# Where the first tiles of x are transposed: tile 1 moved from a transposing load to TensorE, the first loads spread over two queues, and the transposing loads of tiles 2 and 3 put behind a wait

## The chip, the cores and the metric

The kernel runs on one core of a Trainium2 chip. The metric is the device time of one execution in microseconds (us); lower is better. Before the change the median of three runs is 273.49 us (273.46 to 273.66).

## What is computed

One block of a network over 2048 tokens of width 640: a linear attention with 32 heads of width 20 (A), a gated feed-forward of width 1728 (B), and a gate per token that mixes both. All inputs are bfloat16.

```python
def _A_ref(x, wqkv, wo):
    B, S, D = x.shape                      # 1, 2048, 640
    H = 32; Dh = D // H
    qkv = (x @ wqkv).reshape(B, S, 3, H, Dh).transpose(2, 0, 3, 1, 4)
    q, k, v = qkv[0], qkv[1], qkv[2]
    phi = lambda t: jnp.where(t > 0, t + 1, jnp.exp(t)) + 1e-6
    pq, pk = phi(q), phi(k)
    kv = jnp.einsum("bhsd,bhse->bhde", pk, v)
    z = jnp.einsum("bhsd->bhd", pk)
    num = jnp.einsum("bhqd,bhde->bhqe", pq, kv)
    den = jnp.einsum("bhqd,bhd->bhq", pq, z)[..., None] + 1e-6
    return (num / den).transpose(0, 2, 1, 3).reshape(B, S, D) @ wo

def _B_ref(x, w_gate, w_up, w_down):
    return (_gelu(x @ w_gate) * (x @ w_up)) @ w_down

g = _sigmoid((x * gate_w).sum(-1, keepdims=True))
out = g * _A_ref(x, wqkv, wo) + (1 - g) * _B_ref(x, w_gate, w_up, w_down)
```

## The kernel before

The tokens are cut into 16 tiles of 128 (`i`, 0 to 15), and the width of 640 into 5 chunks of 128 (`k`, 0 to 4). TensorE contracts over the 128 partitions, so it needs x with the width on the partitions: `xT`, a buffer of 5 chunks by 2048 tokens. `x_aug` holds x as it lies in memory, tokens on the partitions; it is read later, by the products that sum over the tokens.

The program is written through a small planner. `P.op(engine, function, reads, writes)` appends an instruction to one engine's list, in the order of the calls, and works out which semaphores it must wait for from the resources that it reads and writes. Each engine runs its list strictly in order, and a DMA is an entry of the list of the engine that issues it: "sp" by default, "act" where it is said. An SP instruction that waits holds every later DMA of SP back. SP's DMAs and ACT's DMAs form two queues (q1 and q10 in the profile).

**The loads, in SP's order (L368 to L400).** `load_x(i)` is a plain load of one tile into `x_aug`, `load_wk(k)` a plain load of one chunk of the key weights (both 160 KB, issued at L343), `load_xT(i)` a transposing load of one tile straight into `xT` (L355), `load_wq(k)` a chunk of the query weights. Before: SP issues x0, wk0, xT1, wk3, wk4, xT2, xT3, the five wq, xT4 to xT15, then the rest of x into `x_aug` in two bulk loads, the feed-forward weights and others. ACT issues a tiny load (L368), wk1, wk2, then runs one Exp (which loads its table) and issues the load of the gate vector. `load_xT` already has a parameter `after`, resources that must be there before it is issued; before, nobody passes it.

**NXN** is the number of tiles that are loaded plainly and transposed by TensorE: tile 0 alone. `T(i, ks, tb)` (L435) transposes chunks `ks` of tile i into PSUM bank `tb` with one matmul each against an identity (L439) and copies them to `xT` on DVE (L443). It is called twice a tile, for chunk 0 and for chunks 1 to 4, so that the product with chunk 0 may start after the first, small copy (`r_xTa`).

**The first stage on TensorE (L510 to L534).** `warm(count, n)` issues matmuls of constants whose result nobody reads (bank 4). `KM(n, ks)` (L451) multiplies chunks `ks` of tile n by the key weights, per chunk one matmul of 512 columns (L459) and one of 128 (L460), into the two PSUM banks of slot n (`SLOTS`: banks 0 and 1, 2 and 3, 4 and 5, 6 and 7). `gate_col()` puts the gate vector beside the query weights (one tiny matmul, L504, and a copy). The order is T(0), then KM of tile 0 for chunks 0 to 2, of tile 1 for chunks 0 to 2, both for chunk 3, the gate, both for chunk 4; then tile 2, tile 3, and `QM`, the query products of tiles 0 to 3. `phi1` (ACT, L484) and `phi2` (DVE, L494 and L498) turn each slot into the features.

**Afterwards** `KQ(i)` (L537) does keys and queries of tiles 4 to 15 (matmuls at L544), `MM` (L594) the sums over tokens (L601 to L617), `G` (L694) the feed-forward with the attention's small products between, and `O_tile` and its relatives (L826 to L886) the output.

Of the kernel before, what the change touches and what calls it, by code (L numbers as in the profile page):

```python
# [16 lines left out]
KC = D // 128  # L17
# [3 lines left out]
EPS = 1e-6  # L21
XW = 656

NXN = 1
NQ = 4


# [135 lines left out]
def bass_gated_mix__linear_attn_block__geglu_ffn__prompt_kernel(  # L163
# [63 lines left out]
    with (  # L227
# [8 lines left out]
        with contextlib.ExitStack() as stack:  # L236
# [12 lines left out]
            def new_dma_key():  # L249
                k = "in%d" % dma_next[0]  # L250
                dma_next[0] += 1
                return k
# [16 lines left out]
            wk = wkq[:, :, 0:640]  # L269
# [38 lines left out]
            r_xT = [P.sb("xT%d" % i, R_XT, R_XT + KC * S) for i in range(NT)]  # L308
            r_xTa = [P.sb("xTa%d" % i, R_XT, R_XT + S) for i in range(NXN)]
            r_wk = [P.sb("wk%d" % k, R_WK + k * WW, R_WK + k * WW + 640) for k in range(KC)]  # L310
# [31 lines left out]
            def dma_in(dst, src, writes, reads=(), eng="sp"):  # L342
                P.op(eng, lambda e, dst=dst, src=src: e.dma_start(dst, src),  # L343
                     reads=reads, writes=writes, dma=new_dma_key())
# [3 lines left out]
            def load_x(i, eng="sp"):  # L348
                dma_in(x_aug[:, i, 0:640], A_x[0, i * 128:(i + 1) * 128, :], [r_xn[i]], eng=eng)

            def load_wk(k, eng="sp", after=()):
                dma_in(wk[:, k, :], A_wqkv[k * 128:(k + 1) * 128, 640:1280], [r_wk[k]], reads=after, eng=eng)

            def load_xT(i, after=()):
                P.op("sp", lambda e: e.dma_start_transpose(xT[:, :, i * 128:(i + 1) * 128],  # L355
                                                           A_x[0, i * 128:(i + 1) * 128, :]),
                     reads=list(after), writes=[r_xT[i]], dma=new_dma_key())

            def load_wq(k, eng="sp"):
# [8 lines left out]
            P.op("act", lambda e: e.dma_start(touch[0:16, 0:4], A_wqkv[0:128:8, 640:644]),  # L368
                 writes=[P.res("touch")], dma=new_dma_key())
            load_x(0)  # L370
            load_wk(0)
            load_xT(1)
            load_wk(3)
            load_wk(4)
            load_wk(1, "act")
            load_wk(2, "act")

            zero = nc.const_aps.tensor(0.0, (128, 1), F32)
            P.op("act", lambda e: e.activation(eg[:, 0:1], zero, ACT.Exp), writes=[r_eg[0]])
            P.op("dve", lambda e: e.memset(gw_sb, 0.0), writes=[r_gw])  # L380
            dma_in(gw_sb[0:5, :], gate_w.rearrange("(k p) -> k p", p=128), [r_gw], eng="act")
            for i in range(2, NQ):
                load_xT(i)
            for k in range(KC):
                load_wq(k)
            for i in range(NQ, NT):
                load_xT(i)
            dma_in(x_aug[:, NXN:8, 0:640],
                   A_x[0, NXN * 128:8 * 128, :].rearrange("(i p) w -> p i w", p=128), r_xn[NXN:8])
            dma_in(x_aug[:, 8:NT, 0:640],  # L390
# [30 lines left out]
            def warm(count, n):  # L421
                def fn(e):
                    last = None
                    for w in range(count):
                        last = e.matmul(ps[:, 4, 0:n], one_l, one_r[:, 0:n], start=True, stop=True)
                    return last
                P.op("pe", fn, writes=[bank[4]])
# [4 lines left out]
            def slot(n):  # L432
                return SLOTS[n % 4]

            def T(i, ks, tb):  # L435
                def fn(e):
                    last = None
                    for n, k in enumerate(ks):
                        last = e.transpose(psb[:, tb, n * 128:(n + 1) * 128],  # L439
                                           x_aug[:, i, k * 128:(k + 1) * 128], ident)  # L440
                    return last
                P.op("pe", fn, reads=[r_xn[i], r_ident], writes=[bank[tb]])
                P.op("dve", lambda e: e.tensor_copy(  # L443
                    xT[:, ks[0]:ks[-1] + 1, i * 128:(i + 1) * 128],
                    psb[:, tb, 0:len(ks) * 128].rearrange("p (k s) -> p k s", k=len(ks))),
                    reads=[bank[tb]], writes=[r_xTa[i] if ks[0] == 0 else r_xT[i]])
# [1 line left out]

            seq = [("k", i) for i in range(NQ)] + [("q", i) for i in range(NQ)]

            def KM(n, ks):  # L451
                i = seq[n][1]
                b0, b1 = slot(n)

                def fn(e):
                    last = None
                    for k in ks:
                        lhs = xT[:, k, i * 128:(i + 1) * 128]
                        e.matmul(ps[:, b0, :], lhs, wk[:, k, 0:512], start=(k == 0), stop=(k == KC - 1))  # L459
                        last = e.matmul(ps[:, b1, 0:128], lhs, wk[:, k, 512:640],  # L460
                                        start=(k == 0), stop=(k == KC - 1))
                    return last
                P.op("pe", fn, reads=[r_xTa[i] if i < NXN and ks == [0] else r_xT[i]] + [r_wk[k] for k in ks],
                     writes=[bank[b0], bank[b1]])

            def QM(n, ks):
                i = seq[n][1]
                b0, b1 = slot(n)

                def fn(e):  # L470
                    last = None
                    for k in ks:
                        lhs = xT[:, k, i * 128:(i + 1) * 128]
                        e.matmul(ps[:, b0, :], lhs, wq[:, k, 0:512], start=(k == 0), stop=(k == KC - 1))  # L474
                        last = e.matmul(ps[:, b1, 0:129], lhs, wq[:, k, 512:641],
                                        start=(k == 0), stop=(k == KC - 1))
                    return last
                P.op("pe", fn, reads=[r_xT[i], r_gcol] + [r_wq[k] for k in ks],
                     writes=[bank[b0], bank[b1]])

            def phi1(n):
                b0, b1 = slot(n)
                m = n % 4
                P.op("act", lambda e: e.activation(e_buf[m], ps_flat[:, b0 * 512:b0 * 512 + 640], ACT.Exp),  # L484
                     reads=[bank[b0], bank[b1]], writes=[r_e[m]])
                kind, i = seq[n]
                if kind == "q":
                    P.op("act", lambda e: e.activation(eg[:, i:i + 1], ps[:, b1, 128:129], ACT.Tanh, scale=0.5),
                         reads=[bank[b1]], writes=[r_eg[i]])

            def phi2(n):
                b0, b1 = slot(n)
                m = n % 4
                P.op("dve", lambda e: e.tensor_scalar(e_buf[m], e_buf[m], 1.0, EPS, ALU.min, ALU.add),  # L494
                     reads=[r_e[m]], writes=[r_e[m]])
                kind, i = seq[n]
                dst, r_dst = (pk[i], r_pk[i]) if kind == "k" else (pq[i], r_pq[i])
                P.op("dve", lambda e: e.scalar_tensor_tensor(  # L498
                    dst, ps_flat[:, b0 * 512:b0 * 512 + 640], 1.0 + EPS, e_buf[m], ALU.add, ALU.max),
                    reads=[bank[b0], bank[b1], r_e[m]], writes=[r_dst])  # L500

            def gate_col():

                P.op("pe", lambda e: e.matmul(ps[:, 7, 0:5], gw_sb, ident[:, 0:5], start=True, stop=True),  # L504
                     reads=[r_gw, r_ident], writes=[bank[7]])
                P.op("dve", lambda e: e.tensor_copy(wq[:, :, 640:641], ps[:, 7, 0:5].unsqueeze(2)),
                     reads=[bank[7]], writes=[r_gcol])
# [3 lines left out]
            T(0, [0], 7)  # L511
            T(0, [1, 2, 3, 4], 6)
            warm(1, 512)
            for k in range(3):
                KM(0, [k])
            for k in range(3):
                KM(1, [k])
            KM(0, [3])
            KM(1, [3])
            gate_col()  # L520
            KM(0, [4])
            KM(1, [4])
            ALLK = list(range(KC))
            for n in range(2 * NQ):
                if n in (2, 3):
                    KM(n, ALLK)
                if n == NQ:
                    for k in ALLK:
                        QM(NQ, [k])
                        QM(NQ + 1, [k])  # L530
                if n > NQ + 1:
                    QM(n, ALLK)
                phi1(n)
                phi2(n)  # L534
# [409 lines left out]
```

## Time and profile before

| | us |
|---|---|
| median of three runs | 273.49 (273.46 to 273.66) |
| the profiled execution | 273.48 |
| its span, first to last instruction | 272.2 |

Busy time of the engines in stretches of the span, from the profiled execution:

| stretch, us | what | TensorE busy | DVE busy | ACT busy | GB/s moved |
|---|---|---|---|---|---|
| 0 to 3 | first loads, warm matmuls | 2.17 | 0.11 | 0.80 | 83 |
| 3 to 4 | T(0) | 1.00 | 0.23 | 0.69 | 323 |
| 4 to 5 | first key chunks | 0.81 | 0.42 | 0.00 | 284 |
| 5 to 7 | key chunks of tiles 0 and 1 | 1.78 | 0.00 | 0.00 | 233 |
| 10.8 to 16.4 | query chunks of tiles 0 to 3 | 5.60 | 4.04 | 2.90 | 147 |
| 16.4 to 48.9 | KQ, tiles 4 to 15 | 32.29 | 28.84 | 17.43 | 283 |
| 48.9 to 272.2 | all the rest | 220.12 | 104.82 | 52.12 | 51 |

The granted TensorE clock is 1.00 in all of them. Busy time is what an engine's instructions cover; matmuls overlap, so a busy TensorE is one that always has a matmul in flight. In the names of the views "PE" is TensorE, "PEld" its weight load, "SPq" and "ACTq" the issue of a DMA on SP and ACT, L343 the line, "pool" the kernel's one SBUF buffer, "ps" PSUM, and in_A_x_dram and in_A_wqkv_dram the inputs x and the attention's weights.

Time from issue to landing of the loads of the first stage (start of the issue on its queue, then the profile's time to landing):

| load | queue | issued | to landing |
|---|---|---|---|
| x0 | SP | 0.79 | 2.2 |
| wk0 | SP | 1.26 | 3.0 |
| tile 1, transposing | SP | 1.71 | 3.8 |
| wk3 | SP | 3.07 | 3.5 |
| wk4 | SP | 3.68 | 3.3 |
| tile 2, transposing | SP | 4.15 | 3.9 |
| tile 3, transposing | SP | about 5.4 | 3.3 |
| wq0 to wq4 | SP | 6.72 to 8.8 | 2.5, 2.8, 2.7, 3.0, 3.4 |
| tile 4, transposing | SP | 9.23 | 3.8 |
| wk1, wk2 | ACT | 1.24 and about 1.7 | 3.2 (median of both) |

### The profile page before, as it was taken

What the parts mean: (1) busy time and instruction counts of PE and PEld (TensorE: products, weight loads), DVE (VectorE), ACT (ScalarE), POOL (GpSimd) and SP (SyncE); (2) the same over time, 40 slices, a digit from 0 to 9 for tenths busy, and PEclk for the clock granted to TensorE, in tenths of its full rate; (3) what the DMA queues carried; (4) which work ended last, traced back from release to release, by engine and by line L of the source; (5) the groups of instructions that cost most, each with busy time, mean ns of one, the idle gap of its engine ahead of it and who ended that gap; (6) DMA issues with size and microseconds to landing.
All of it is one profiled execution on the core that took longest, in us unless ns stands there. A gap on an engine that the chain in (4) does not pass through costs nothing.

```text
span 272.2 us, 3460 instructions
## 1 busy us (share of the span) xinstructions
PE 267.3 (98%) x1365; PEld 127.0 (47%) x1391; DVE 141.0 (52%) x248; ACT 75.9 (28%) x132; POOL 30.6 (11%) x30
## 2 busy tenths in 40 slices
PE   8999999999999999999999999999999999999997
PEld 3555555544445454444444444444444444444444
DVE  1678989997234335999999999634110000000200
ACT  2455555210422453332222232224011122121021
POOL 6000000003240002242332421000000000000000
PEclk9999999999999999999999999999999999999999
DMA  7976999610200011615121221272031110110221
GB/s 189 202 117 126 348 401 381 116 8 19 58 19 2 23 52 48 199 27 48 28 48 30 45 48 25 60 235 92 2 78 40 39 39 19 40 39 19 58 60 39
DMA packets 42680, 23.61 MB, mean 87 GB/s; under 512 B 32167, under 2 KB 41255, under 8 KB 42535
## 3 DMA queue, kind: packets, MB, share of 16 engines
q1 hardware_dynamic: 42333, 23.05, 32.4%
q10 hardware_dynamic: 330, 0.33, 0.4%
q8 instruction: 11, 0.18, 0.3%
q14 instruction: 6, 0.05, 0.1%
HBM read 13.67 MB, written 2.63 MB: 60 GB/s over the span
## 4 chain that ended last, share of the span: by engine, by line
PE 96%; DMA 1%; SPq 1%; issue 1%; DVE 0%
PE ps L705 41%; PE ps L879 23%; PE ps L544 12%; PE ps L601 6%; PE ps L858 4%; PE ps L683 2%; PE ps L474 2%; PE ps L826 2%; PE ps L604 1%; DMA pool<-in_A_x_dram 1%; PE ps L459 1%; PE ps L839 1%; SPq L343 1%; SPq L355 0%; PE ps L754 0%
## 5 line engine op out<-in xcount | busy, mean ns | idle before, releaser
L705 PE MATMUL ps<-pool 128*128 128x512 bf16 x509 | 112.8, 379 | 0.7 <-issue 0.2
L705 PEld LDWEIGHTS ps<-pool 128*128 128x128 bf16 x520 | 50.5, 98 | 60.3
L879 PE MATMUL ps<-pool 128*128 128x512 bf16 (+2 forms) x300 | 62.2, 366 | 0.5 <-issue 0.2
L711 ACT ACTIVATE pool<-ps 128x512 f32<-128x512 f32 x52 | 31.0, 597 | 72.8 <-PE ps L705 70.1
L713 DVE TENSOR_TENSOR pool<-ps,pool 128x512 bf16<-128x512 f32 x52 | 34.7, 689 | 31.1 <-PE ps L705 29.8
L879 PEld LDWEIGHTS ps<-pool 128*128 128x128 bf16 x306 | 29.1, 98 | 33.5 <-issue 0.4
L862 DVE TENSOR_TENSOR pool<-ps,pool 128x512 bf16<-128x512 f32 x4 | 2.8, 692 | 61.5 <-PE ps L858 59.4
L544 PE MATMUL ps<-pool 128*128 128x512 bf16 (+1 forms) x176 | 32.5, 343 | 0.2
L769 POOL TENSOR_TENSOR pool<-pool 128x640 f32<-128x640 bf16 x16 | 22.4, 1404 | 72.6 <-DVE pool L771 65.5
L886 ACT ACTIVATE pool<-ps,pool 128x512 bf16<-128x512 f32 (+1 forms) x16 | 10.9, 680 | 68.6 <-PE ps L879 68.6
L544 PEld LDWEIGHTS ps<-pool 128*128 128x128 bf16 x180 | 17.6, 98 | 15.0
L563 DVE SCALAR_TENSOR_TENSOR pool<-ps,pool 128x128 bf16<-128x128 f32 (+2 forms) x36 | 21.7, 603 | 2.1
L554 ACT ACTIVATE pool<-ps 128x640 bf16<-128x640 f32 x24 | 16.9, 703 | 15.8 <-DVE pool L563 9.4
L601 PE MATMUL ps<-pool 128*128 128x512 bf16 x76 | 19.2, 379 | 0.1
L779 DVE TENSOR_TENSOR pool<-pool 128x640 bf16<-128x640 bf16 x16 | 13.2, 825 | 0.6
L777 DVE TENSOR_SCALAR pool<-pool 128x32 f32<-128x32 f32 x16 | 12.8, 802 | 0.6
L771 DVE TENSOR_REDUCE pool<-pool 128x32 f32<-128x640 f32 x16 | 12.9, 808 | 0.0
L649 DVE TENSOR_TENSOR pool<-pool 128x640 f32<-128x640 f32 x14 | 11.6, 826 | 0.5
L858 PE MATMUL ps<-pool 128*128 128x512 bf16 x51 | 11.4, 379 | 0.0
L651 POOL PARTITION_ALL_REDUCE pool<-pool x1 | 4.0, 3971 | 60.2 <-DVE pool L649 60.2
L601 PEld LDWEIGHTS ps<-pool 128*128 128x128 bf16 x78 | 7.0, 98 | 7.3
L560 DVE TENSOR_SCALAR pool<-pool 128x640 bf16<-128x640 bf16 x24 | 7.9, 327 | 1.7 <-ACT pool L554 0.4
(73 smaller groups left out, 123.6 us busy)
## 6 DMA issues: line engine op xcount, KB each, us to landing
out_dram<-pool SPq DMA_DIRECT2D x19, 128.0 KB, 1.7
pool<-in_B_w_gate_dram SPq DMA_DIRECT2D x1, 2080.0 KB, 14.0
pool<-in_B_w_up_dram SPq DMA_DIRECT2D x1, 2080.0 KB, 18.1
pool<-in_A_wqkv_dram SPq DMA_DIRECT2D x8, 160.0 KB, 3.0
pool<-in_A_x_dram SPq DMA_DIRECT2D x1, 1280.0 KB, 9.1
pool<-in_A_x_dram SPq DMA_DIRECT2D x1, 1120.0 KB, 6.2
pool<-in_B_w_down_dram SPq DMA_DIRECT2D x1, 1120.0 KB, 6.2
pool<-omg_row SPq DMA_DIRECT2D x1, 1024.0 KB, 4.5
```

The costliest lines, as they stand in the source:

```text
L544: last = e.matmul(ps[:, b + p, 0:c1 - c0], xT[:, k, i * 128:(i + 1) * 128], wkq[:, k, c0:c1], start=(k == 0), stop=(k == KC - 1))
L554: P.op("act", lambda e: e.activation(e_buf[m], ps_flat[:, o:o + 640], ACT.Exp), reads=banks, writes=[r_e[m]])
L563: P.op("dve", lambda e, c0=c0, c1=c1: e.scalar_tensor_tensor(dst[:, c0:c1], ps_flat[:, o + c0:o + c1], 1.0 + EPS, e_buf[m][:, c0:c1], ALU. ...
L601: last = e.matmul(ps[:, b, :], pk[i][:, c * 128:(c + 1) * 128], x_aug[:, i, 0:512], start=(i == 0), stop=(i == NT - 1))
L705: last = e.matmul(ps[:, b, :], w[:, k, fc * 128:(fc + 1) * 128], xT[:, k, j * 512:(j + 1) * 512], start=(k == 0), stop=(k == KC - 1))
L711: P.op("act", lambda e: e.activation(ge[n], ps[:, gb, :], ACT.Gelu_apprx_tanh), reads=[bank[gb]], writes=[r_ge[n]])
L713: P.op("dve", lambda e: e.tensor_tensor(hT[fc][:, j * 512:(j + 1) * 512], ps[:, ub, :], ge[n], ALU.mult), reads=[bank[ub], r_ge[n]], write ...
L769: P.op("pool", lambda e: e.tensor_tensor(tmp[n], pq[i], z_b, ALU.mult), reads=[r_pq[i], r_zb], writes=[r_tmp[n]])
L771: P.op("dve", lambda e: e.tensor_reduce(den[n], tmp[n].rearrange("p (h d) -> p h d", h=32), AX.X, ALU.add), reads=[r_tmp[n]], writes=[r_de ...
L779: P.op("dve", lambda e: e.tensor_tensor(pq[i].rearrange("p (h d) -> p h d", h=32), pq[i].rearrange("p (h d) -> p h d", h=32), den[n].unsqu ...
L858: last = e.matmul(ps[:, b, :], wd[:, fc, 512:640], hT[fc][:, j * 512:(j + 1) * 512], start=False, stop=(fc == NFC - 2), skip_group_check=True)
L879: last = e.matmul(ps[:, pb, 0:c1 - c0], lhs, rhs, start=False, stop=(q == len(rows) - 1), skip_group_check=True)
```

## The change

`NXN` becomes 2: tile 1 is loaded plainly into `x_aug`, and TensorE transposes it (two calls of T, banks 5 and 4). Its transposing load goes; the bulk load of `x_aug` starts at tile 2. SP issues x0, wk0, wk2, wk4; ACT issues the tiny load, x1, wk1, wk3. The transposing loads of tiles 2 and 3 now wait for wk0 to have landed before SP issues them; the query chunks and all else on SP come after them as before. On TensorE two short warm matmuls are added, and the chunks of tiles 0 and 1 are taken in the order 0, 2, 1, 4, 3, with T(1) after the first chunk of tile 0; the stop flag of the accumulation goes to the last chunk in the new order, so `KM` has a new parameter.

```diff
--- before.py
+++ after.py
@@ -21,7 +21,7 @@
 EPS = 1e-6
 XW = 656
 
-NXN = 1
+NXN = 2
 NQ = 4
 
 
@@ -368,19 +368,19 @@
             P.op("act", lambda e: e.dma_start(touch[0:16, 0:4], A_wqkv[0:128:8, 640:644]),
                  writes=[P.res("touch")], dma=new_dma_key())
             load_x(0)
+            load_x(1, "act")
             load_wk(0)
-            load_xT(1)
-            load_wk(3)
+            load_wk(1, "act")
+            load_wk(2)
+            load_wk(3, "act")
             load_wk(4)
-            load_wk(1, "act")
-            load_wk(2, "act")
 
             zero = nc.const_aps.tensor(0.0, (128, 1), F32)
             P.op("act", lambda e: e.activation(eg[:, 0:1], zero, ACT.Exp), writes=[r_eg[0]])
             P.op("dve", lambda e: e.memset(gw_sb, 0.0), writes=[r_gw])
             dma_in(gw_sb[0:5, :], gate_w.rearrange("(k p) -> k p", p=128), [r_gw], eng="act")
-            for i in range(2, NQ):
-                load_xT(i)
+            for i in range(NXN, NQ):
+                load_xT(i, [r_wk[0]])
             for k in range(KC):
                 load_wq(k)
             for i in range(NQ, NT):
@@ -448,7 +448,7 @@
 
             seq = [("k", i) for i in range(NQ)] + [("q", i) for i in range(NQ)]
 
-            def KM(n, ks):
+            def KM(n, ks, last_chunk):
                 i = seq[n][1]
                 b0, b1 = slot(n)
 
@@ -456,9 +456,9 @@
                     last = None
                     for k in ks:
                         lhs = xT[:, k, i * 128:(i + 1) * 128]
-                        e.matmul(ps[:, b0, :], lhs, wk[:, k, 0:512], start=(k == 0), stop=(k == KC - 1))
+                        e.matmul(ps[:, b0, :], lhs, wk[:, k, 0:512], start=(k == 0), stop=(last_chunk and k == ks[-1]))
                         last = e.matmul(ps[:, b1, 0:128], lhs, wk[:, k, 512:640],
-                                        start=(k == 0), stop=(k == KC - 1))
+                                        start=(k == 0), stop=(last_chunk and k == ks[-1]))
                     return last
                 P.op("pe", fn, reads=[r_xTa[i] if i < NXN and ks == [0] else r_xT[i]] + [r_wk[k] for k in ks],
                      writes=[bank[b0], bank[b1]])
@@ -511,19 +511,21 @@
             T(0, [0], 7)
             T(0, [1, 2, 3, 4], 6)
             warm(1, 512)
-            for k in range(3):
-                KM(0, [k])
-            for k in range(3):
-                KM(1, [k])
-            KM(0, [3])
-            KM(1, [3])
-            gate_col()
-            KM(0, [4])
-            KM(1, [4])
+            warm(2, 128)
+            KM(0, [0], False)
+            T(1, [0], 5)
+            T(1, [1, 2, 3, 4], 4)
+            KM(0, [2], False)
+            for k in (0, 2, 1, 4, 3):
+                if k in (1, 4, 3):
+                    KM(0, [k], k == 3)
+                KM(1, [k], k == 3)
+                if k == 4:
+                    gate_col()
             ALLK = list(range(KC))
             for n in range(2 * NQ):
                 if n in (2, 3):
-                    KM(n, ALLK)
+                    KM(n, ALLK, True)
                 if n == NQ:
                     for k in ALLK:
                         QM(NQ, [k])
```

## The prediction

> **What bounds the kernel now.** I read the page first, parts 1 and 4: is one engine full, and does the chain that ended last run through it?
>
> ```profile
> PE 267.3 (98%) x1365; PEld 127.0 (47%) x1391; DVE 141.0 (52%) x248; ACT 75.9 (28%) x132; POOL 30.6 (11%) x30
> ...
> PE 96%; DMA 1%; SPq 1%; issue 1%; DVE 0%
> ```
>
> TensorE is busy nearly always and 96% of the chain is its own work. The few per cent that aren't lie at the start, so I read the chain of waits in order of time up to 8.6 us (start, length, what).
>
> ```profile
> 0.79 0.41 SPq L343
> ...
> 1.26 0.41 SPq L343
> ...
> 1.71 1.30 SPq L355
> ...
> 3.07 0.57 SPq L343
> ...
> 3.68 0.43 SPq L343
> ...
> 4.15 3.88 DMA pool<-in_A_x_dram
> ...
> 8.07 0.39 PE ps L459
> ```
>
> The reader is to see that the chain is SP's queue: it issues x0, wk0, the transposing load of tile 1 (1.30 us of issuing against 0.41 for a plain load), wk3 and wk4, and only at 4.15 the transposing load of tile 2. That lands after 3.88 us, and at 8.07 the key product of tile 2 begins. From there TensorE never waits again: the 10 key chunks of tiles 2 and 3 run 8.07 to 10.80, so 0.273 each, and the query chunks follow. So the time changes by as much as the start of tile 2's product moves, unless tile 3 or a query chunk becomes late.
>
> The timeline of TensorE up to there shows its other waits (start, length, instruction, then the idle time of the weight load and its releaser).
>
> ```profile
> 4.34 0.10 PEld L459 LDWEIGHTS ps<-pool 128*128 128x128 bf16 x1 [0.50 <-DVE pool L443]
> ...
> 5.54 0.10 PEld L459 LDWEIGHTS ps<-pool 128*128 128x128 bf16 x1 [0.52 <-DMA pool<-in_A_x_dram]
> ...
> 6.56 0.10 PEld L459 LDWEIGHTS ps<-pool 128*128 128x128 bf16 x1 [0.36 <-DMA pool<-in_A_wqkv_dram]
> ...
> 8.07 0.10 PEld L459 LDWEIGHTS ps<-pool 128*128 128x128 bf16 x1 [0.56 <-DMA pool<-in_A_x_dram]
> ```
>
> The first is put down to the copy of L443, but its two copies began at 3.69 and took 0.23 and 0.43, so the small one was done by 3.92; what came last was wk0, issued at 1.26 and landed 3.0 later, at 4.26. The next is tile 1's transposing load (issued 1.71, 3.8 to land: 5.5), then wk3 (3.07, 3.5: 6.6), then tile 2.
>
> How far could any change of this stage go? From 4.37 on, 20 key chunks at 0.273, five transposes (about 0.45, below) and the gate column (0.03, L504 to the next matmul at 7.12 and 7.15) are 5.94 us: query chunks at 10.31 instead of 10.80. **Without a single wait the gain is 0.5 us**; if the first chunk also started when the small copy ends, 3.92 plus some 0.07, 0.9 us.
>
> **The change part by part.**
>
> *Transposing load of tile 1 taken out.* SP has 1.30 + 0.05 us less to issue, and tile 1 no longer waits until 5.5.
>
> *Plain x1 and the key chunks on two queues.* SP issues x0, wk0, wk2, wk4 at about 0.79, 1.26, 1.71, 2.16; ACT issues x1, wk1, wk3 at about 1.24, 1.69, 2.15, with x1 where wk1 stood. ACT's table load slips from 2.20 to about 2.65 and the gate vector's load with it; ACT then sat idle 3.9 us before its first L484 at 7.62, which hides it. Seven loads of 160 KB (163.8 kB) are 1.15 MB. The windows say 83 GB/s over the first 3.0 us, 0.25 MB; the other 0.90 MB go at 323 GB/s (window 3 to 4, both queues filled) in 2.8 us, last byte at 5.8. Each queue gets half if they share evenly, one load per 1.0 us. With wk0 where it landed before (4.26; its own queue has the same ahead of it) and x1 where wk1 landed (1.24 + 3.2 = 4.44), estimates are wk2 5.25, wk4 6.25, wk1 5.45, wk3 6.45.
>
> *Tile 1 transposed by TensorE (T(1), five transposes), two copies by DVE, two more warm matmuls.* The row of L439 has five in 0.62, before 3.96; one 128-column matmul among the key chunks costs 0.055 at best. So five cost 0.28 to 0.62; I take 0.45, five weight loads of 0.10 less a little, because the load of 0.10 is longer than 0.055 and each transpose has its own. The copies cost 0.23 and 0.43 and start 0.35 after their first transpose (3.34 to 3.69); DVE was idle for 2.93 us before 7.36, so they delay nobody but the chunks of tile 1. The two warm matmuls, about 0.1, lie before wk0 lands.
>
> *New order of the chunks.* KM(0,0) 4.37 to 4.64; T(1) (x1 there at 4.44) to 5.09, small copy done 5.3, large one 5.85; KM(0,2) at 5.28 for wk2, to 5.55; KM(1,0) to 5.82; KM(1,2) after the copy 5.9 to 6.17; then KM(0,1), KM(1,1), KM(0,4), KM(1,4), gate, KM(0,3), KM(1,3): 6 x 0.273 + 0.03 to **7.84**. Each of wk1, wk4, wk3 is there 0.5 to 0.8 before its use. Before, the last of these chunks began at 7.42 and TensorE was free at 7.7; so tile 0 and 1 end about 0.15 later, in the shade of the 8.07. If that shade went, it is 7.84 that would set the start of tile 2.
>
> *The transposing loads of tiles 2 and 3, now behind a wait for wk0.* SP is through with its plain loads at 2.6 and then waits for wk0, to 4.26 + 0.05. Queued behind the wait on SP are both transposing loads, all five query chunks, tiles 4 to 15 and every later load; TensorE waits for the first. So tile 2 is issued at 4.31 against 4.15 before: the 1.5 us saved on SP are all spent waiting. From issue to landing the first three transposing loads took 3.8, 3.9 and 3.3; the first two, like the one to come, had plain chunks ahead of them. In the new order wk4 is some 0.2 us from its end when the descriptors of tile 2 are out (4.31 + 1.30 = 5.6), somewhat less than before, so I take 3.75 with 3.3 and 4.6 (the shortest of the first three, and the longest of all 15) as bounds: landing at **8.06**, bounds 7.6 and 8.9. Tile 3 is issued at 5.65, lands at 8.95 to 9.5 (3.3 to 3.85), and is needed 5 x 0.273 after 8.08, at 9.45. The query chunks are issued 0.16 later each; they landed at 9.2 to 12.1 (6.72 + 2.5 to 8.75 + 3.4) and are used from 10.80 to 12.98, 0.9 or more of slack. Tile 4 (9.23 + 3.8 = 13.0) is used at 16.42.
>
> One row about the price of a transposing load: with the transposing loads of tiles 2 and 3 in the queue the DMA moved less, with plain loads only more.
>
> ```profile
> 7.00:8.00 1.00, 0.85 (x8) 0.33 (x5) 0.18 (x1) 0.38 (x1) 0.00 (x0) 1.00 1.05 160
> 8.00:10.50 2.50, 2.37 (x17) 1.36 (x19) 2.08 (x4) 1.62 (x3) 0.00 (x0) 1.00 0.93 266
> ```
>
> The last numbers are GB/s: 160 and 266. [...]
>
> *The bulk load of x_aug* (1120 KB at 25.5 us) loses one tile; the products that read it begin at 48.9.
>
> Sum: tile 2's product starts at 8.08 instead of 8.07, nothing after it waits: 273.48 of the profiled execution + 0.0 = **273.5 us**. That execution's span is 272.2, 1.3 lie around it, and the median of the runs is 273.49, so no correction.
>
> **The rivals.**
>
> *No wait is left (272.8).* If wk0 lands earlier because no transposing load is being issued in the same microseconds, say at 3.9, SP's wait ends earlier too, tile 2 lands at 3.95 + 3.3 to 3.75, so 7.3 to 7.7, and TensorE's chain decides, itself begun up to 0.4 earlier: 7.4 against 8.07, 272.8. For it: the window of 0 to 3 moved only 83 GB/s, so there is room. Against: wk0 shares the DMA with ACT's first load as before, and x1's landing holds T(1).
>
> *The wait costs more than the load it removes (274.3).* The mechanism is SP held by wk0 with both transposing loads behind it. It decides once tile 2 lands after 8.6, which takes wk0 at 4.8 or a landing time of 4.35. At the longest row, 4.6, tile 2 is there at 8.91, 0.84 late: 274.3; tile 3 at 5.65 + 4.6 = 10.25 would alone cost 0.7. For it: three of the 15 took 4.2 or more by the list of issues, the issue begins later than before by 0.16, and more plain traffic stands on the other queue. Against: those long ones had other transposing loads ahead of them.
>
> *x1 comes late on ACT's queue (274.0 to 274.1).* If it lands as the second load of that queue would (5.45), T(1) ends at 5.9, its large copy at 6.65, the chunks at 8.6: +0.53. Against: wk1 in that place landed at 4.44.
>
> *Transposes are dearer than the row of T(0) (274.1).* The single instructions of L439 last 0.22 to 0.31; if they did not overlap, five would take 1.1 to 1.5, some 0.85 more than taken, the chunks would end at 8.7 and the time would be 0.6 longer. Against: the five of T(0) took 0.62 together, at the slow pace of the first microseconds. [...]
>
> **How the numbers follow.** A measurement of this kernel tells about 0.2%, 0.55 us, from no change. My case, within it (272.94 to 274.04): 0.55. No wait left: 0.15, all faster. SP's wait: 0.20, x1 late beyond 0.55: 0.08, dear transposes: 0.02, all slower, 0.30. The range leaves out the best of the first rival and the worst of the second: 272.9 to 274.3.
>
> **What would show it.** Right: SP's tile 2 load issued at about 4.3 with nothing before it since 2.6; the chunks of tile 0 and 1 done at 7.8; tile 2's first matmul at 8.0 to 8.2 with a DMA of in_A_x as releaser. The first rival shows as tile 2 following with no idle time before it. Wrong steps would be wk0 away from 4.26, T(1) over 0.62, tile 2 over 4.3 to land, or a wait before tile 3 or a query chunk.

## The result and the profile after

| | before | after |
|---|---|---|
| median of 22 runs each, us | 273.56 (273.28 to 274.17) | 274.00 (273.54 to 274.99) |
| ratio to before, 95% interval | | 1.0019 [1.001, 1.0027] |
| the profiled execution, us | 273.48 | 274.99 |
| its span, us | 272.2 | 273.7 |

The change costs 0.44 us in the median. That is inside the 0.2% within which I counted a result as "no change", but the interval leaves 1 out: the loss is small and real. The profiled execution of after is the slowest of its 22. So I had the unchanged kernel profiled once more (label c1_again below, 273.86) and read that one as the usual case.

Page of after, busy time of the engines and the chain that ended last:

```profile
PE 269.8 (99%) x1398; PEld 128.0 (47%) x1398; DVE 141.2 (52%) x250; ACT 75.9 (28%) x132; POOL 30.5 (11%) x30
...
PE 96%; DMA 2%; DVE 1%; SPq 0%; issue 0%; ACT 0%; DVEq 0%
```

TensorE is still the bound. DVE has two instructions more (250 against 248, the copies of T(1)); ACT has the same 132 activations, and one DMA issue more, which the page does not count. Both will matter.

The chain of waits of this execution, 0 to 7 us (start, length, what):

```profile
0.79 0.41 SPq L343
...
1.26 0.41 SPq L343
...
1.71 4.99 DMA pool<-in_A_wqkv_dram
...
6.84 0.38 PE ps L459
```

The chain no longer runs through a transposing load. It runs through wk2: issued at 1.71 as foreseen, landed 4.99 later, at 6.70 instead of the 5.25 of my sum. TensorE's weight loads beside it (start, length, instruction, then the idle time before it and who ended it):

```profile
4.94 0.57 PEld L439 LDWEIGHTS ps<-pool 128*128 128x128 bf16 x5 [0.28 <-DMA pool<-in_A_x_dram]
6.80 0.10 PEld L459 LDWEIGHTS ps<-pool 128*128 128x128 bf16 x1 [1.29 <-DVE pool L443]
```

The five transposes of tile 1 are loaded by 5.5; then TensorE's weight loads stand for 1.29 us before KM(0, [2]). They are put down to DVE, but the small copy began at 5.39 and was long done: it is wk2, as the chain says. Tile 2, on SP's queue issued at 4.38, landed after 4.0, at 8.4, while TensorE reached it only at 9.25. Its landing decided nothing.

In the second profile, of the same kernel, the same views read differently:

```profile
1.26 3.35 DMA pool<-in_A_wqkv_dram
4.61 0.14 issue
4.74 0.38 PE ps L459
```

```profile
4.96 0.32 PEld L439 LDWEIGHTS ps<-pool 128*128 128x128 bf16 x5
5.57 0.10 PEld L459 LDWEIGHTS ps<-pool 128*128 128x128 bf16 x1 [0.29 <-DVE pool L443]
...
11.06 0.10 PEld L474 LDWEIGHTS ps<-pool 128*128 128x128 bf16 x1 [0.18 <-DVE pool L498]
...
12.53 0.10 PEld L474 LDWEIGHTS ps<-pool 128*128 128x128 bf16 x1 [0.26 <-DMA pool<-in_A_wqkv_dram]
```

wk0 lands at 4.61, wk2 some 3.75 after its issue, at 5.46, and from 5.57 on TensorE runs chunk after chunk without a wait. Tile 2's first chunk is loaded at 8.01, the first query chunk at 10.73 (before: 10.75). Then come two waits that before did not have: 0.18 for the features of DVE and 0.26 for a query chunk. All that follows begins 0.11 us later than before. This execution, though, was 0.38 longer than before's. **The other 0.25 us arise at 49 us**, far from everything that was edited, at the head of MM (the sums over tokens); of the 1.51 by which the slowest execution is longer, 1.23 come from the start and 0.25 from this same place.

### The profile page after: what moved, and what is told of

The parts are those of the page before. It is cut to its first block, busy times and chain, and to the rows that moved or that the text cites. A ratio compares the mean times of both kernels' runs of the same rounds, so it can differ in the third digit from the quotient of the medians.

```text
span 273.7 us, 3502 instructions
## 1 busy us (share of the span) xinstructions
PE 269.8 (99%) x1398; PEld 128.0 (47%) x1398; DVE 141.2 (52%) x250; ACT 75.9 (28%) x132; POOL 30.5 (11%) x30
## 4 chain that ended last, share of the span: by engine, by line
PE 96%; DMA 2%; DVE 1%; SPq 0%; issue 0%; ACT 0%; DVEq 0%
PE ps L707 41%; PE ps L881 23%; PE ps L546 11%; PE ps L603 6%; PE ps L860 4%; DMA pool<-in_A_wqkv_dram 2%; PE ps L474 2%; PE ps L685 2%; PE ps L828 2%; PE ps L459 2%; PE ps L606 1%; PE ps L841 1%; PE ps L756 0%; PE ps L475 0%; PE ps L460 0%; PE ps L732 0%
```

## The experiments

"Late by" below is the start of ACT's instructions against those of the profiled execution of before: once at 28 us, after the first stage, and once at 269 us, just before the end. A change between the two is time lost or won in the middle. Intervals are 95%.

**The unchanged kernel again, without the wait, on one queue, and with before's split.** c1 is after itself. e1 takes only the wait for wk0 out:

```diff
-                load_xT(i, [r_wk[0]])
+                load_xT(i)
```

e2 takes the wait out and issues all seven plain loads on SP, leaving out ACT's tiny first load; e3 takes the wait out and keeps before's order of key chunks:

```diff
 e2, SP alone:  load_x(0) load_wk(0) load_x(1) load_wk(2) load_wk(1) load_wk(4) load_wk(3)
 e3, SP:        load_x(0) load_wk(0) load_wk(3) load_wk(4)
 e3, ACT:       load_x(1) load_wk(1) load_wk(2)
```

> The changed kernel once more, unaltered, for a second profile. Late loads (my theory): the chunks wk2 and wk1 land after the 5.25 and 5.45 that I had reckoned, since a load is there only when the slowest of its parts is, and the first long wait of TensorE after tile 1's transposes is for one of these chunks; how late differs from execution to execution, so this profile should have wk2 between 5.3 and 6.7 and a time between 273.6 and 274.9. Rival, SP's wait: the chunks are on time, the wait is ahead of tile 2, at 8.2 or later. Rival, TensorE's own work: no wait over 0.2 at all, and the chunks of tiles 0 and 1 end after 8.1.

> The changed kernel with the transposing loads of tiles 2 and 3 not waiting for wk0. Late loads: the plain loads are the same and stand ahead of the transposing ones in the queue, so nothing is won: within 0.2 us of the changed kernel, 274.0, with tile 2 issued at 2.6 and landing when wk4 has, about 7.5. SP's wait (rival): 273.5, as before the change. The wait helps (second rival): the transposing loads now compete with the chunks, 274.4 or more.

> The changed kernel with all seven plain loads on SP in the order of their use (x0, wk0, x1, wk2, wk1, wk4, wk3), none on ACT, the tiny first load of ACT left out, and no wait for wk0. Late loads, from sharing between two queues: with one queue each load has all the bandwidth in turn (0.6 us each at 266 GB/s), x1 lands at about 4.2, wk2 4.8, wk1 5.4, wk4 6.0, wk3 6.6; tile 2 issued at 3.95, there at 7.8 or so; 273.3 to 273.6. If the sharing is not the cause and the amount of plain data is: 274.0 as the changed kernel. SP's wait (rival): 273.5 as well, but then without the wait alone the time comes back too.

> Tile 1 through TensorE as in the changed kernel, but the key chunks on the queues that they had before (SP: x0, wk0, wk3, wk4, then tiles 2 and 3 with no wait; ACT: x1, wk1, wk2) and the chunk order of before, with T(1) after the first chunk. Late loads: the same seven plain loads share the two queues, wk2 is third on ACT and lands at 6 or later; 273.9 to 274.3. SP's wait: 273.5 or less. TensorE's own work (rival): 274.0 whatever the split.

| run | median | ratio | late by at 28 us | late by at 269 us |
|---|---|---|---|---|
| c1_again | 273.94 | 1.0018 [1.0008, 1.0028] | 0.11 | 0.36 |
| e1_no_gate | 273.94 | 1.0015 [1.0006, 1.0024] | -0.06 | 0.19 |
| e2_one_queue | 273.99 | 1.0016 [1.0007, 1.0025] | 0.48 | 0.47 |
| e3_split_of_before | 274.69 | 1.0040 [1.0027, 1.0054] | 0.81 | 1.05 |

The wait is not the loss: without it the median is the same. The two single profiles differ by 0.17 at the start (0.11 against -0.06). With the wait SP issues the query chunks from 7.30 on, without it from 5.3 on, and the wait of 0.26 at 12.53 is gone; but wk0 also landed at 4.40 in e1 and at 4.61 in c1, so the 0.17 is not shown to be the wait's, and the medians do not show it. With all plain loads on one queue the median is the same too (273.99, 273.94), but it is made up in another way: e2 starts 0.48 late and loses nothing afterwards. That late start does not come from the loads (wk0 landed at 3.58, against 4.26 before); TensorE's chain ran at its slow pace until about 6.5, as in k1 below. What one queue wins or loses against two, these medians do not show, since e2 differs from e1 in its order of loads and in ACT's list as well. e3 is slower for a plain reason: wk2 goes third on ACT's queue, lands at 6.62, and the chunk that needs it is the third to run.

What c1, e1 and e3 share is the last column: each loses another 0.24 to 0.25 us after 28 us, whatever its first stage did; e2 doesn't. In DVE's timeline at 34 to 36 us there is a place where after and before differ. First before, then c1:

```profile
34.37 0.33 DVE L560 TENSOR_SCALAR pool<-pool 128x640 bf16<-128x640 bf16 x1
34.80 0.82 DVE L563 SCALAR_TENSOR_TENSOR pool<-ps,pool 128x640 bf16<-128x640 f32 x1
```

```profile
34.48 0.33 DVE L562 TENSOR_SCALAR pool<-pool 128x640 bf16<-128x640 bf16 x1
35.33 0.83 DVE L565 SCALAR_TENSOR_TENSOR pool<-ps,pool 128x640 bf16<-128x640 f32 x1 [0.52 <-DVE pool L562]
```

The same instruction of the features of keys and queries starts 0.43 after its predecessor before, and 0.85 after it now, with an idle time of 0.52 that is put down to DVE's own last instruction: a gap without a cause in the profile. It stands before the same instruction in after, c1, e1, e2 and e3, all kernels with two DVE instructions more ahead of it.

**Is it the gap, and is it the number of DVE instructions?** f1 is before with two tiny memsets added early to DVE's list. f2 is after with the two copies of T(1) given to ACT, so that DVE's list is again as long as before's; f3 is f2 without the wait.

```diff
 f1, on before:
+            for n in range(2):
+                P.op("dve", lambda e, n=n: e.memset(touch[:, 8 + 4 * n:12 + 4 * n], 0.0), writes=[r_pad])
 f2, on after:
+                if i == 0:
+                    P.op("dve", lambda e: e.tensor_copy(dst, src), reads=[bank[tb]], writes=w)
+                else:
+                    P.op("act", lambda e: e.activation(dst, src, ACT.Copy), reads=[bank[tb]], writes=w)
```

> The kernel before with two tiny memsets of unused columns added at the start of DVE's list, so that every later DVE instruction stands where it stands in the changed kernel; nothing reads them and DVE is idle then. If the gap of 0.52 us that the changed kernels show on DVE at 35 us (and the kernel before does not) comes from the place of the instruction in DVE's list: the same gap appears before the same instruction, the sums over tokens wait for DVE for about 0.6 instead of 0.2, and the time is 273.75, 0.25 more than before. If the gap comes from the loads or from the later chunks of tiles 0 and 1: no gap, 273.5.

> The changed kernel with the two copies of T(1) on ACT in place of DVE, so that DVE's list is as long as before. Place in DVE's list: no gap on DVE at 35 us, the sums over tokens wait as before, 273.7 (274.0 less 0.25; what is left, 0.1 to 0.2, is the first stage). Loads or late chunks: the gap stays, 274.0. The copies last a little longer on ACT, which may delay one chunk of tile 1 by up to 0.2.

> As the last, and with no wait for wk0 ahead of the transposing loads. Place in DVE's list: no gap, 273.45, about the kernel before, since without the wait the tiles from 4 on started 0.06 earlier than before the change. Loads or late chunks: as the changed kernel without the wait, 273.9.

| run | median | ratio | late by at 28 us | late by at 269 us |
|---|---|---|---|---|
| f1_before_two_memsets | 273.59 | 1.0001 [0.9993, 1.0010] | -0.34 | -0.35 |
| f2_copies_on_act | 273.73 | 1.0005 [0.9997, 1.0014] | 0.01 | 0.00 |
| f3_copies_on_act_no_gate | 273.65 | 1.0011 [0.9998, 1.0024] | 0.04 | 0.03 |

f2 and f3 have no gap and lose nothing after 28 us. But f1 has the gap, in the same place, and loses nothing: my theory that the gap alone costs 0.25 fell.

```profile
34.03 0.33 DVE L563 TENSOR_SCALAR pool<-pool 128x640 bf16<-128x640 bf16 x1
34.88 0.82 DVE L566 SCALAR_TENSOR_TENSOR pool<-ps,pool 128x640 bf16<-128x640 f32 x1 [0.52 <-DVE pool L563]
```

So I compared what f1 and c1 do between 35 and 50 us. In c1 ACT has a late start of its own. Before and c1, ACT's timeline, then DVE's, for each:

```profile
47.18 0.70 ACT L554 ACTIVATE pool<-ps 128x640 bf16<-128x640 f32 x1 [0.78 <-DVE pool L563]
```

```profile
46.79 1.02 DVE L563 SCALAR_TENSOR_TENSOR pool<-ps,pool 128x128 bf16<-128x128 f32 x2
47.91 0.33 DVE L560 TENSOR_SCALAR pool<-pool 128x640 bf16<-128x640 bf16 x1
```

```profile
47.70 0.70 ACT L556 ACTIVATE pool<-ps 128x640 bf16<-128x640 f32 x1 [1.20 <-PE ps L546]
```

```profile
47.01 1.02 DVE L565 SCALAR_TENSOR_TENSOR pool<-ps,pool 128x128 bf16<-128x128 f32 x2
48.44 0.33 DVE L562 TENSOR_SCALAR pool<-pool 128x640 bf16<-128x640 bf16 x1 [0.41 <-ACT pool L556]
```

What releases this activation is the first of DVE's two 128x128 instructions. Before, ACT starts 0.39 after that one's start (46.79, 47.18); in c1 0.69 after it (47.01, 47.70), 0.3 too late, and DVE's next instruction stands 0.41 for ACT. The profile names TensorE (PE) as the releaser in c1, but the last entry ahead of this activation is a wait for DVE's semaphore, met at 47.35, and the activation starts 0.35 after that. Against before, DVE is 0.53 late at 35 us (34.80, 35.33), has worked that down to 0.22 at 47 us (46.79, 47.01), and is 0.53 late again at its next instruction (47.91, 48.44). In f1 DVE does not stand there. The late start is found in every kernel so far with one entry more in ACT's list (after, c1, e1, e3: x1's load is issued there), one tile later in e2, where ACT's list is shorter than before's, and not in before, f1, f2 and f3.

**Both gaps, one by one.** g1 is after with two tiny activations added to ACT's list: the DVE gap should stay and the late start of ACT go. g3 is before with two memsets on DVE and one activation on ACT: both should appear in a kernel whose loads and order are before's.

```diff
 g1, on after (g3: on before, range(1), and the two memsets of f1):
+            for n in range(2):
+                P.op("act", lambda e, n=n: e.activation(touch[:, 4 + n:5 + n], zero, ACT.Copy),
+                     writes=[P.res("apad%d" % n)])
```

> The changed kernel with two tiny activations of a constant into unused columns, early in ACT's list (ACT is idle then); DVE's list is left alone. The changed kernels have one entry more on ACT than the kernel before (one more load), and one activation of tile 14 starts 0.40 after its release where all others take 0.10; with three more entries (the copies of T(1) on ACT) that delay is gone. Place in the lists: DVE's gap of 0.52 at 35 us stays, ACT's late start at 47 to 48 us goes, the sums over tokens wait 0.3 for DVE and not 0.6, and the time is 273.75, 0.25 less than the changed kernel. If DVE's gap alone is the cost: 274.0. If both are without weight and all is the first stage: 274.0 too, but with ACT's late start gone.

> The kernel before, its loads and products untouched, with two tiny memsets at the start of DVE's list and one tiny activation at the start of ACT's, so that both lists are as long ahead of the tiles as in the changed kernel. Place in the lists: DVE's gap at 35 us and ACT's late start at 47 us both appear, the sums over tokens wait about 0.6 for DVE, and the time is 273.8, 0.25 more than the kernel before. First stage alone (rival): 273.55 as before.

| run | median | ratio | DVE gap | ACT late | late by at 28 us | late by at 269 us |
|---|---|---|---|---|---|---|
| g1_after_two_act | 273.57 | 1.0001 [0.9992, 1.0010] | yes | no | -0.02 | -0.03 |
| g3_before_two_dve_one_act | 273.68 | 1.0009 [1.0000, 1.0017] | yes | yes | 0.12 | 0.37 |

**With two useless activations added, the changed kernel loses nothing after 28 us**, and three useless instructions in the kernel before bring the step of 0.25 into it. The median of g1 is 0.37 to 0.43 below those of the changed kernel, more than this step: its profile also starts 0.13 earlier at 28 us than c1's (-0.02, 0.11; wk0 landed at 4.26 and not 4.61), which the two activations are not shown to do. In the median g3 is 0.18 slower, just clear of noise; its step of 0.25 stands in its one profile. The weight loads at the head of MM in before, c1, g1 and g3 show how:

```profile
49.22 0.10 PEld L616 LDWEIGHTS ps<-pool 128*128 128x128 bf16 x1 [0.16 <-DVE pool L563]
49.40 0.15 PEld L601 LDWEIGHTS ps<-pool 128*128 128x128 bf16 x2
```

```profile
49.75 0.10 PEld L618 LDWEIGHTS ps<-pool 128*128 128x128 bf16 x1 [0.58 <-DVE pool L565]
49.77 0.15 PEld L603 LDWEIGHTS ps<-pool 128*128 128x128 bf16 x2
```

```profile
49.30 0.10 PEld L621 LDWEIGHTS ps<-pool 128*128 128x128 bf16 x1 [0.26 <-DVE pool L568]
49.38 0.15 PEld L606 LDWEIGHTS ps<-pool 128*128 128x128 bf16 x2
```

```profile
49.75 0.10 PEld L622 LDWEIGHTS ps<-pool 128*128 128x128 bf16 x1 [0.57 <-DVE pool L569]
49.77 0.15 PEld L607 LDWEIGHTS ps<-pool 128*128 128x128 bf16 x2
```

Weight loads run ahead of the matmuls (before: the weights loaded at 49.22 are those of the matmul of 49.40), so a wait of 0.16 or 0.26 is made up by the next line (49.40 and 49.38). One of 0.58 is not: the next product loads at 49.77, of the 0.37 more than before 0.11 were brought along from the first stage, and 0.26 stay to the end. Until then DVE could work off a gap of 0.42, having some idle time left (c1: 0.53 late at 35 us, 0.22 at 47); with ACT's 0.3 on top it did not.

That the late starts move and vanish with the number of entries in the engine's list, and not with what the entries do, is shown. The traces even give the number. Count all that an engine has in the trace, waits and DMA issues included: the late instruction is the 64th record of its engine in every one of the nine profiles with the DVE gap and of the seven with the late start of ACT (after, c1, e1, e2, e3, g3, e4). In all of them the 63rd is a wait, and the 64th starts 0.45 to 0.47 after it on DVE and 0.35 on ACT; at the other such places between 17 and 53 us, in before, c1, g1 and e4, it is 0.04 to 0.05. Where nothing starts late, the 63rd is no wait but an instruction of work; a delay of the 64th that runs while that one works would not show. The 128th shows no such delay (in after, on DVE and on ACT, it starts 0.02 us after the signal that released it), so this is no rule for every 64 records. What the engine does at that place is not shown.

**What the first stage would lose without the transposes on TensorE.** e4 is before with one plain load of x1 more, on ACT's queue; h1 is before with wk3 moved from SP to ACT, and two activations to keep ACT's list clear of the late start. Both leave tile 1 to its transposing load.

```diff
 e4, on before:
             load_wk(4)
+            load_x(1, "act")
             load_wk(1, "act")
 h1, on before:
             load_xT(1)
-            load_wk(3)
             load_wk(4)
             load_wk(1, "act")
             load_wk(2, "act")
+            load_wk(3, "act")
```

> The kernel before, with one more plain load: x1, 160 KB, on ACT ahead of wk1 and wk2. Nobody needs it early (the bulk load writes the same tile again later, with a wait that has long been met). Traffic of the first stage as a cost by itself: wk1 lands at about 5.4 and wk2 at 5.9 or later in place of 4.4 and 4.9, the chunks of tiles 0 and 1 end at about 8.3, and tile 2 lands later by up to 0.3 behind the same traffic; 273.8. If only the place in DVE's list matters, which this leaves alone: 273.5.

> A try at a faster one: the kernel before (tile 1 by a transposing load, no new wait), with only wk3 moved from SP to the end of ACT's queue, and two tiny activations so that ACT's list doesn't run into its late start. SP issues tile 2 at 3.5 and not at 4.15. If the start of tile 2 sets the time and nothing else is late: tile 2 lands at 7.4, its product starts at 7.5 to 7.6, query chunks at 10.3 to 10.4, 273.1. If the plain loads on ACT now hold each other up as in the changed kernel (wk3 at 6.5 or later): 273.4 to 273.6.

Measured: e4 275.09, ratio 1.0073 [1.0048, 1.0097]; h1 274.73 (274.03 to 276.85), ratio 1.0052 [1.0029, 1.0075]. Both lose far more than one plain load takes on its queue (about 1.0 us in the prediction's sharing). h1's profiled execution (276.85) is the slowest of its nine, 2.1 above the median, e4's (275.42) is near its own. (e4 also has one entry more on ACT and shows what the late start costs without the gap on DVE: late by 1.76 at 28 us and 1.90 at 269 us, so 0.14.) The chain of e4 and its weight loads, then those of h1:

```profile
2.20 5.37 DMA pool<-in_A_wqkv_dram
```

```profile
5.58 0.10 PEld L460 LDWEIGHTS ps<-pool 128*128 128x128 bf16 x1 [1.03 <-issue]
...
7.61 0.10 PEld L460 LDWEIGHTS ps<-pool 128*128 128x128 bf16 x1 [1.89 <-DMA pool<-in_A_wqkv_dram]
```

```profile
1.72 6.11 DMA pool<-in_A_x_dram
```

```profile
5.81 0.10 PEld L462 LDWEIGHTS ps<-pool 128*128 128x128 bf16 x1 [1.04 <-DMA pool<-in_A_wqkv_dram]
...
7.87 0.10 PEld L462 LDWEIGHTS ps<-pool 128*128 128x128 bf16 x1 [1.94 <-DMA pool<-in_A_x_dram]
...
8.28 0.15 PEld L462 LDWEIGHTS ps<-pool 128*128 128x128 bf16 x1 [0.28 <-issue]
```

With three plain loads on ACT's queue instead of two, the transposing load of tile 1, issued at 1.72 as before, takes 6.1 to land instead of 3.8; in e4 it takes 5.7 (there at 7.46), and wk2, now third on ACT, 5.4 (there at 7.57). So in h1 it is the transposing load that TensorE waits for last, in e4 the plain wk2. e3 has the same seven plain loads on the same queues without the transposing load of tile 1 among them, and wk2 landed at 6.62 there. TensorE stands 1.04 and 1.94 us in h1, and then it goes at half its clock; in e4 it stands 1.03 and 1.89, and the clock stays. Windows of h1 and of e4 (stretch, length, busy time of PE, PEld, DVE, ACT, POOL, then the granted clock, DMA share and GB/s):

```profile
7.00:8.00 1.00, 0.13 (x1) 0.13 (x2) 0.00 (x0) 0.00 (x0) 0.00 (x0) 0.94 1.19 220
8.00:10.00 2.00, 2.00 (x9) 0.90 (x8) 0.00 (x0) 0.00 (x0) 0.00 (x0) 0.50 1.16 331
```

```profile
8.00:10.00 2.00, 2.00 (x18) 1.10 (x15) 0.18 (x1) 0.25 (x1) 0.00 (x0) 1.00 1.16 325
```

The half clock is thus not what these medians lost: the mean granted clock lies below 1 (0.994) in two of nine executions of h1 and in one of six of e4.

This speaks for the one thing in the change that is worth having: with one plain load more on ACT's queue, the transposing load of tile 1 came 1.9 to 2.3 us later than before, and in e4 a plain one came late too, while in c1 x1 landed at 4.8 and was transposed in time. Each is one profile.

**A version that might beat both.** k1 is g1 without the wait, and with KM(1, [0]) ahead of KM(0, [2]), so that wk2 has 0.27 us more.

> The best that the runs so far point to: the changed kernel with two tiny activations early in ACT's list, without the wait for wk0, and with tile 1's chunk 0 taken ahead of tile 0's chunk 2, which in the last profile without the wait held TensorE for 0.4. Place in the lists: no late start on ACT, the sums over tokens wait 0.3 or less. First stage: query chunks at 10.5 to 10.7 in place of 10.80. Together 273.3 to 273.45, 0.1 to 0.2 below the kernel before. If chunk wk2 is as late as in the first profile of the changed kernel, it is still above 274 in single executions. Nothing gained: 273.55.

Measured: 273.69 (273.16 to 274.05), ratio 1.0002 [0.9993, 1.0011]: nothing won. Its profiled execution was late by 0.46 at 28 us and by 0.46 at the end, so the middle is clean, with 0.27 of waiting at MM's head. The 0.46 come from TensorE itself, whose chain reads without any wait from the first matmul on:

```profile
5.14 0.11 PE ps L463
5.25 0.53 PE ps L442 x5
5.78 0.50 PE ps L462
6.28 0.11 PE ps L463
6.39 0.31 PE ps L462
6.71 0.06 PE ps L463
6.76 0.22 PE ps L462
```

Up to 6.3 a 128-column matmul adds 0.11 to the chain, from the last row but one on 0.06: until there TensorE was at its slow pace of the first microseconds, though the granted clock of the profile reads 1.00 from 5.0 to 6.3 as well. In c1 that ended before 5, in the slowest execution of after after 5 (five weight loads in 0.57 against 0.32), though it is the same kernel. So the first stage has a spread of some tenths of a microsecond that the order of the work does not set.

## Why the prediction was right, and where it was not

The number was right: 274.0 lies in 272.9 to 274.3, and in the case that I gave 0.55. That it lies there is partly luck: it is 0.04 inside that case's upper edge of 274.04, the sum said no change where 0.44 was measured, clear of noise, and the profiled execution (274.99) is outside the whole range. The way there was half wrong.

- **"Nothing after it waits" and "they delay nobody" failed**, and with them the zero of the sum. I costed DVE's two copies and ACT's one DMA issue by their duration and what they delay nearby. Their price was their place: two entries in DVE's list and one in ACT's move later instructions to places where they start 0.42 and 0.3 late, and together these cost 0.25 us at 49 us. In every kernel where they start late it is the 64th record of the engine, right behind a wait. Shown by g3, where 0.12 grows to 0.37 with before's loads and order, and by g1, f2 and f3, whose profiles lose nothing after 28 us. The rest of the 0.44 lies in the first stage (0.11 in c1's profile), which varies between executions. No row of before could have shown it; the sign could have been left open.
- **"Tile 2's landing sets the start" failed.** It was issued at 4.62 in the usual profile (I had 4.31) and landed at 7.46, earlier than TensorE came to it. That is 2.84 after its issue, where I had taken 3.75 and 3.3 as the lower bound, so this term of the sum was mis-sized as well. In the slowest execution it took 3.97. What decides is TensorE's own chain, the 7.84 that I had put in the shade. Loaded at 8.01, tile 2 began as foreseen (8.08) for another reason: the chain started 0.37 later, since wk0 landed at 4.61 and not 4.26, and was 0.2 shorter.
- **Even sharing of the loads** held in the usual profile: wk2 took 3.75 (landed 5.46, said 5.25), wk1 and wk4 3.9, wk3 4.1. In the slowest execution the term was mis-sized: wk2 4.99, so 6.70, and TensorE waited 1.29. There, of the 16 signals that tell of wk2's landing, 15 had come by 5.51 us and the last came at 6.70; for wk1, wk4 and wk3 the last came 1.24, 1.41 and 1.33 after the 15th. Six of 33 executions of after lie above 274.5, none of the 49 of before measured beside them; the one that was profiled has this cause, the other five have no profile, and why the last signal lagged is open.
- **T(1), 0.45** was right: five weight loads in 0.32 at the full pace, 0.57 at the slow one. The dear transposes did not come. A single one lasts 0.22 to 0.31 here, but that is not the price of one in a row: they overlap, and five in c1 took 0.44 of TensorE's time, from 5.01 to 5.45.
- **SP's wait** stood on SP as foreseen, at 2.6 to 4.4 or 4.6. Taking it out changed nothing in the median (273.94 both). But "0.9 or more of slack" for the query chunks failed: by the prediction's own figures it was 12.98 - 12.15 less 0.16, so 0.67 for the last one, and in c1 they were issued 0.58 later, the fourth took 3.6 to land instead of 3.0, and it kept TensorE for 0.26.
- **The rivals.** "No wait is left" showed its sign, tile 2 with no idle time before it, and not its price, because wk0 came later instead of earlier. "SP's wait costs" would have needed tile 2 after 8.6; not seen. "x1 late" did not come: 3.6 to land on ACT's queue, at 4.8, with T(1) right behind the first chunk. (In the rival on SP's wait, tile 3 alone would have cost 0.8 by its own figures, 10.25 - 9.45, and not 0.7.) The loss is of the size that the last rivals had, from a place that none of them named.

## What to carry to other kernels

When a small edit to a tuned kernel costs a few tenths of a microsecond, compare both traces to the end, not only where the edit is: note when some fixed instruction starts against its twin, and see at which time the distance changes. If it changes far from the edit, pad the lists of the engines that the edit lengthened with a few empty instructions, before giving the edit up or keeping it. Here it was enough to look at which record of each engine's list is the 64th and whether it stands right behind a wait: one entry more on ACT's list brought the late start, three more did not. And look twice at a plain load added to the other queue beside a transposing load that something waits for: in this kernel it cost 1.2 to 1.5 us (h1, e4).

## What the runs showed of the hardware that was not expected

- An instruction can start late (0.42 on DVE, 0.3 on ACT) with nothing in the profile that it waited for, at a place that depends on how many entries stand ahead of it in its engine's list: seen in nine profiles of nine with two more on DVE (after, c1, e1, e2, e3, f1, g1, g3, k1), and in none of the five with DVE's list at its old length (before, e4, f2, f3, h1). In each of them it is the 64th record of the engine, and the 63rd is a wait. Two tiny memsets and one tiny activation bring both late starts into before (g3); two tiny activations take ACT's out of the changed kernel (g1).
- A transposing load landed after 3.8 us beside two plain loads of 160 KB on the other queue (before), and after 5.7 and 6.1 beside three (e4, h1). The plain loads suffer as well: wk2, third on ACT in both, landed at 7.57 in e4 and at 6.62 in e3, which lacks that transposing load. Why, no run isolates.
- TensorE's clock fell to 0.50 after standing 1.04 and 1.94 us with one chunk between (h1), and stayed so from 8 us to about 11. In e4's profile two waits of nearly that length (1.03 and 1.89) with one chunk between left it at 1.00 throughout, so from what length of wait on the clock falls, and what else decides it, is not shown.
- The slow pace at the start (five weight loads took 0.57 in after against 0.32 in c1; a 128-column matmul added 0.11 to k1's chain, later 0.06) ended at different times, from before 4 us (before) and 5 us (c1) to about 6.3 us (k1) and 6.5 us (e2), also in two executions of one kernel (c1 and after).
